# First block's second product on float16 halves, three more steps turned by TensorE, three more copies of V on chip, in a chain of linear attention, FFN and expert FFN

## The chip, the cores and the metric

The program runs on one core of one Trainium2 chip. The metric is the device time of one execution in microseconds: 719.73 us, median of three runs (719.59 to 719.96). Five engines matter: TensorE (PE; its weight loads are shown apart as PEld), VectorE (DVE), ScalarE (ACT), GpSimd (POOL) and SyncE (SP, which issues nearly all transfers).

## The reference

```python
for t in range(S):                       # attention, B=4 H=8 S=768 D=48
    cur = einsum('bhd,bhe->bhde', u * k[t], v[t])
    y[t] = einsum('bhd,bhde->bhe', r[t], state + cur)
    state = w * state + einsum('bhd,bhe->bhde', k[t], v[t])
x = y as [3072, 384]
h = x @ w_in                             # 384 -> 2048
g = maximum(h, 0) + log1p(exp(-abs(h)))
x = g @ w_out                            # 2048 -> 384
logits = x @ w_gate                      # 8 experts, 384 places each, greedy by logit
for e: out[mask_e] = maximum(x[mask_e] @ w1[e], 0) @ w2[e]
```

w_in and w_out arrive as float64 and are turned into float32 on chip.

## The kernel before

**Stages.** The 3072 tokens are 24 attention steps of 128 tokens (two batches of 64 positions), and every three steps make a block of 384 tokens for the FFN, so there are 8 blocks. `attention(n)` scales r and k by powers of w, turns them (L588), multiplies (L615), masks, adds the state (L646 to L660) and writes its 128 rows of x to `xf`. For the FFN x has to stand turned, in `XT`. Steps 0 to 2 are turned by TensorE into float32. The other steps write float16 halves of x to `xhl`, which a DMA with transpose turns (L753). V is needed a second time, in `X`, beside the state: steps 0 to 2 do without it (DIRECT), steps 3 to 5 copy it from the loaded tile on ACT or DVE (`n < COPIED`), from step 6 on a second pair of loads fetches it from HBM (L461).

**Products.** `ffn1(blk, f)` makes g of one of 16 pieces of 128 columns, `ffn2(blk, t, f)` adds one such piece to the output of one step. From block 1 on both work on float16 pairs: a value is hi + lo, and a product is three matmuls (hi·hi, hi·lo, lo·hi; L879 and L1010 to L1012). Block 0 is float32 in both products (L872, L1007): its g is kept whole in `G32`, a view of the memory of the halves, and w_out whole in `WU32`, a view of the memory of the halves one place further on. The 392 columns of L1007 are 384 of w_out and 8 of w_out·w_gate, which `prep_wout` makes (turning w_out by L823, multiplying by L835, turning back by L840).

**Weights.** `from_double` loads float64 pieces (L795, L814; two buffers of 768 KB) and rebuilds float32 by three VectorE operations (L786, L788, L790). `halve_win` (L806) and `halve_wout` (L849) then make the halves, which are needed from block 1 on. Since a half of piece f lies where the float32 of piece f-1 was, halving follows the last use of that.

**Order.** All operations go through a planner, `lay_out`: a list scheduler with a cost for each operation, due times (`due_ffn1`, `due_ffn2` and leads such as HALFL2), and `NUDGE`, a table of numbers that shifts the priority of single operations. Its result is the order of each engine's instructions, which then run in order and wait by semaphores. Where the plan leaves TensorE idle, `keep_warm` puts matmuls of a constant tile (L184, bank 7), which compute nothing that is used; here they are called fillers.

```python
            k = int((it.start - last - 100.0) / step)
            if k > 0 and it.start - last > SWITCH + 60.0:
                        PE.matmul(banks[7][:, :128], still, still, start=True, stop=True)
```

Of the kernel before, what the change touches and what calls it, by code (L numbers as in the profile page):

```python
# [21 lines left out]
def tile_kernel(ctx, tc, r, k, v, w, u, w_in, w_out, w_gate, w1, w2, out):  # L22
# [32 lines left out]
    LAT = 150.0  # L55
    SLACK = 87.403
    SAME = {"dve": 130.0, "act": 150.0}
    NBANK = 7
    BIAS = 1.853
    YIELD0 = 218.503  # L60
    YIELD = {"dve": YIELD0}
# [22 lines left out]
    NUDGE = {  # L84
# [24 lines left out]
    }  # L109
# [219 lines left out]
    TURNED = 3  # L329
    DIRECT = 3  # L330
    SUMMED = 0
    SINGLE = 2
    COPIED = 6
    PARTED = 8
    QUEUES = 1
    UDUE = 2000.0
    ZERODUE = 30000.0
    UTDUE = 6000.0
    HALFL = 12965.117
    HALFL2 = 16904.146  # L340
    NLAT = 6
# [37 lines left out]
    G0 = ffn2p.tile([128, 2, FC, BT], HF, name="g0")  # L379
    G32 = G0.rearrange("p a f t -> p (a f t)").bitcast(FT).rearrange("p (f t) -> p f t", f=FC)  # L380
    G = [[G0[:, 0], G0[:, 1]], several(ffn2p, 2, [128, FC, BT], HF, "g1")]
# [171 lines left out]
    def attention(n):  # L553
# [202 lines left out]
        if blk == 0:  # L756
# [3 lines left out]
            return  # L760
        if n < TURNED:
            op("pe", 1300.0 if summed else 321.0, tx, r=xfs + ["ident"], w=[(a, g, t) for a in ("xh", "xl", "x2")], due=due + 5, bank=b6)
            op(FROM_PSUM, 0.0, lambda eng: scaled(eng, hi, b6.view(KC, 128), 64.0), w=[("xh", g, t)], due=due + 5, bank=b6)
            op("dve", 470.0, lambda: DVE.scalar_tensor_tensor(lo, b6.view(KC, 128), 64.0, hi, op0=OP.mult, op1=OP.subtract),
               r=[("xh", g, t)], w=[("xl", g, t)], due=due + 5, bank=b6)
        else:
            xh, xl = XHL[i][:, :DM], XHL[i][:, DM:]
            op(FROM_SBUF, 0.0, lambda eng: scaled(eng, xh, xf, 64.0), r=[("xf", i)], w=[("xhl", i, 0), "rkT"], due=due + 5)
            op("dve", 470.0, lambda: DVE.scalar_tensor_tensor(xl, xf, 64.0, xh, op0=OP.mult, op1=OP.subtract),
               r=[("xf", i), ("xhl", i, 0)], w=[("xhl", i, 1)], due=due + 5)  # L770
            op("sp", 1340.0, turn, r=[("xhl", i, 0), ("xhl", i, 1)], w=[("xh", g, t), ("xl", g, t), ("x2", g, t)], due=due + 5, size=TURN)
# [72 lines left out]
    def halve_wout(f):  # L844
        due = due_ffn2(1, 0, f) - HALFL2
        hi, lo = WU[:, f, 0], WU[:, f, 1]
        op({"act": 420.0, "dve": 273.0}, 0.0, lambda eng: scaled(eng, hi, WU32[f], 512.0), r=[("wo", f + 1), ("wg", f + 1)],
           w=[("wo", f), ("wg", f)], due=due)
        op("dve", 478.0, lambda: DVE.scalar_tensor_tensor(lo, WU32[f], 512.0, hi, op0=OP.mult, op1=OP.subtract),  # L849
           r=[("wo", f), ("wo", f + 1), ("wg", f + 1)], w=[("wol", f)], due=due)  # L850
# [9 lines left out]
    def ffn1(blk, f):  # L860
# [30 lines left out]
        op("act", 413.0, lambda: ACT.activation(ta, ta, AF.Ln, bias=1.0), w=[("ta", c)], due=due)  # L891
        if blk == 0:
            op("dve", 470.0, lambda: DVE.scalar_tensor_tensor(G32[:, f, :], bank.view(BT), 0.0, ta, op0=OP.max, op1=OP.add),
               r=[("ta", c)], w=[("gh", g, f), ("gl", g, f)], due=due, bank=bank)
            return
        op("dve", 470.0, lambda: DVE.scalar_tensor_tensor(gf, bank.view(BT), 0.0, ta, op0=OP.max, op1=OP.add),  # L896
# [96 lines left out]
    def ffn2(blk, t, late=False):  # L993
# [10 lines left out]
        def mm(f):  # L1004
            p = bank.view(no)
            if blk == 0:
                PE.matmul(p, G32[:, f, ts], WU32[f], start=(f == 0), stop=(f == FC - 1))  # L1007
                return
            gh, gl = G[g]
            PE.matmul(p, gh[:, f, ts], WU[:, f, 0, :no], start=(f == 0), stop=False)  # L1010
            PE.matmul(p, gh[:, f, ts], WU[:, f, 1, :no], start=False, stop=False)  # L1011
            PE.matmul(p, gl[:, f, ts], WU[:, f, 0, :no], start=False, stop=(f == FC - 1))  # L1012

        for f in range(FC):
            it = op("pe", 500.0 if blk else 660.0, lambda f=f: mm(f), r=[(a, g, f) for a in ("gh", "gl")]
               + ([("wo", f), ("wg", f), ("wol", f)] if blk else [("wo", f + 1), ("wg", f + 1)]),
               due=base + 490.0 * (late_n * FC + f) if late else due_ffn2(blk, t, f), bank=bank)
            if blk == 0:
                G0R.append(it)
        scale = 2.0 ** -12 if blk else 4.0  # L1020
        due = base if late else due_ffn2(blk, t, FC - 1)
# [39 lines left out]
    for blk in range(2, NB):  # L1061
        for n in range(blk * SPB, (blk + 1) * SPB):
            load_step(n)
            attention(n)
        for t in range(SPB):
            if (blk - 2, t) not in LATE:
                ffn2(blk - 2, t)
        if blk == 2:
            for f in range(FC):
                halve_wout(f)  # L1070
            gates()
# [559 lines left out]
```

## Time and profile before

| | us |
|---|---|
| median of three runs | 719.73 |
| lowest, highest | 719.59, 719.96 |
| the profiled execution | 720.05 |
| span of its trace | 718.2 |

The profile page gives busy time by engine, then the span in 40 slices of 18 us, then the chain of work that ended last and the costliest groups. A matmul's record is longer than the distance to the next one, since matmuls are pipelined, so a TensorE that is shown busy need not be at its peak. What a matmul costs is read from the starts of consecutive ones. A float32 matmul has two records. The granted clock of TensorE was 0.997 of 2.4 GHz over the span.

### The profile page before, as it was taken

To read this page: it belongs to the slowest core of one execution; us is meant where nothing else is said; L and a number is where in the kernel's file an instruction comes from. 1 tells how busy PE (TensorE), PEld (TensorE's weight loads), DVE (VectorE), ACT (ScalarE), POOL (GpSimd) and SP (SyncE) were. 2 spreads that over 40 slices of the span, in tenths; PEclk is the share of its full clock that TensorE was granted. 3 is DMA by queue.
4 is the path that set the end of the run, shared out by engine and by line. 5 is a ranking of instruction groups with operands and counts; after the bars stand their busy time and mean duration, and the time that the engine had idled before them with its cause. 6 is when DMAs were issued, how large, how long until landed. Compare 5 with 4: busy or idle time off the path is not lost.

```text
span 718.2 us, 18288 instructions
## 1 busy us (share of the span) xinstructions
PE 707.8 (99%) x7173; PEld 458.5 (64%) x7173; DVE 604.0 (84%) x1638; ACT 401.7 (56%) x889; POOL 63.4 (9%) x107
## 2 busy tenths in 40 slices
PE   9999999999899999999999999999999999999996
PEld 8986666657666666666666566666666665566663
DVE  6999999999898968988899868887799898988630
ACT  4588698674398712689999801311345533524530
POOL 3000000000000000000010000001212422313211
PEclk9999999999999999999999999999999999999998
DMA  6985972445741426512010003442358667647900
GB/s 120 267 202 155 237 149 38 90 86 116 124 77 23 74 52 127 75 29 43 15 23 1 1 13 111 122 143 57 102 143 212 192 155 201 195 124 210 265 34 33
DMA packets 165015, 79.65 MB, mean 111 GB/s; under 512 B 132801, under 2 KB 158273, under 8 KB 164929
## 3 DMA queue, kind: packets, MB, share of 16 engines
q1 hardware_dynamic: 159216, 68.56, 42.0%
q0 software_dynamic: 3072, 9.44, 3.7%
q8 instruction: 56, 0.92, 0.5%
q10 hardware_dynamic: 2640, 0.49, 0.4%
q14 instruction: 31, 0.25, 0.1%
HBM read 60.37 MB, written 9.83 MB: 98 GB/s over the span
## 4 chain that ended last, share of the span: by engine, by line
PE 64%; DVE 15%; issue 12%; DMA 3%; POOL 3%; ACT 2%; POOLq 0%; SPq 0%; DVEq 0%
PE bank L879 20%; PE bank L1010 6%; PE bank L1012 6%; PE bank L1011 6%; PE bank L1504 6%; PE bank L1007 3%; DVE ar L625 2%; PE bank L720 2%; PE bank L184 2%; PE bank L1522 2%; PE bank L1524 2%; PE bank L1523 2%; POOL out L1532 2%; PE bank L615 1%; PE bank L588 1%
## 5 line engine op out<-in xcount | busy, mean ns | idle before, releaser
L879 PEld LDWEIGHTS <-wi 128*128 128x128 f16 x1008 | 98.0, 98 | 65.3 <-issue 1.1
L879 PE MATMUL bank<-xt,wi 128*128 128x384 f16 x672 | 127.6, 326 | 0.1
L1010 PE MATMUL bank<-wo,g 128*128 128x384 f16 (+1 forms) x240 | 78.5, 327 | 0.0
L1012 PE MATMUL bank<-wo,g 128*128 128x384 f16 (+1 forms) x240 | 78.5, 327 | 0.0
L1011 PE MATMUL bank<-wo,g 128*128 128x384 f16 (+1 forms) x240 | 78.4, 327 | 0.0
L879 PE MATMUL bank<-xs,wi 128*128 128x384 f16 x336 | 72.9, 326 | 0.0
L1504 PE MATMUL bank<-g,w1h 128*128 128x384 f16 x384 | 72.8, 325 | 0.0
L889 ACT ACTIVATE ta<-bank 128x384 f32<-128x384 f32 x128 | 61.5, 481 | 17.2 <-PE bank L879 12.9
L896 DVE SCALAR_TENSOR_TENSOR gf<-bank,ta 128x384 f32<-128x384 f32 x112 | 61.6, 551 | 11.2 <-ACT ta L891 10.0
L891 ACT ACTIVATE ta<-ta 128x384 f32<-128x384 f32 x128 | 66.6, 522 | 1.7
L890 ACT ACTIVATE ta<-ta 128x384 f32<-128x384 f32 x128 | 66.4, 522 | 1.5
L1524 PE MATMUL bank<-w2h,g 128*128 128x384 f16 x192 | 62.6, 326 | 0.0
L1523 PE MATMUL bank<-w2l,g 128*128 128x384 f16 x192 | 62.5, 326 | 0.0
L1522 PE MATMUL bank<-w2h,g 128*128 128x384 f16 x192 | 62.5, 326 | 0.0
L1508 ACT ACTIVATE g<-bank 128x384 f16<-128x384 f32 x64 | 31.2, 489 | 43.1 <-PE bank L1504 29.2
L421 ACT ACTIVATE x2o<-bank 128x384 f16<-128x384 f32 x23 | 11.3, 493 | 72.8 <-PE bank L1012 65.3
L1504 PEld LDWEIGHTS <-w1h 128*128 128x128 f16 x384 | 35.5, 97 | 22.9 <-issue 1.0
L903 DVE SCALAR_TENSOR_TENSOR g<-gf,g 128x384 f16<-128x384 f32 x80 | 43.2, 549 | 2.9 <-ACT g L421 2.2
L1511 DVE SCALAR_TENSOR_TENSOR g<-bank,g 128x384 f16<-128x384 f32 x64 | 34.4, 547 | 11.0 <-ACT g L1508 11.0
L1504 PE MATMUL bank<-g,w1l 128*128 128x384 f16 x192 | 41.7, 326 | 0.0
L625 DVE TENSOR_TENSOR ar<-bank,mask 64x256 f32<-64x256 f32 x84 | 35.4, 421 | 4.5 <-PE bank L615 2.7
L1429 POOL DMA_INDIRECT third<-x2d,idx x24 | 25.1, 1044 | 150.7 <-PE bank L1317 124.8
(251 smaller groups left out, 1403.9 us busy)
## 6 DMA issues: line engine op xcount, KB each, us to landing
mraw<-moe_w SPq DMA_DIRECT2D x64, 384.0 KB
third<-moe_w_out SPq DMA_DIRECT2D x8, 768.0 KB
third<-moe_w_in SPq DMA_DIRECT2D x6, 768.0 KB
x2d<-x2o SPq DMA_DIRECT2D x48, 96.0 KB
vn<-v SPq DMA_DIRECT2D x47, 96.0 KB
rn<-r SPq DMA_DIRECT2D x46, 96.0 KB
kn<-k SPq DMA_DIRECT2D x46, 96.0 KB
X<-v SPq DMA_DIRECT2D x36, 96.0 KB
```

The lines of the kernel that those rows point to most:

```text
L879: PE.matmul(ph, WF[:, f, a, kk, :], x[:, kk, :], start=(i == 0), stop=(i == 3 * KC - 1))
L889: op("act", 371.0, lambda: ACT.activation(ta, bank.view(BT), AF.Abs), w=[("ta", c)], due=due, bank=bank)
L890: op("act", 413.0, lambda: ACT.activation(ta, ta, AF.Exp, scale=-1.0), w=[("ta", c)], due=due)
L891: op("act", 413.0, lambda: ACT.activation(ta, ta, AF.Ln, bias=1.0), w=[("ta", c)], due=due)
L896: op("dve", 470.0, lambda: DVE.scalar_tensor_tensor(gf, bank.view(BT), 0.0, ta, op0=OP.max, op1=OP.add), r=[("ta", c)], w=[("gf", c)], due ...
L1010: PE.matmul(p, gh[:, f, ts], WU[:, f, 0, :no], start=(f == 0), stop=False)
L1011: PE.matmul(p, gh[:, f, ts], WU[:, f, 1, :no], start=False, stop=False)
L1012: PE.matmul(p, gl[:, f, ts], WU[:, f, 0, :no], start=False, stop=(f == FC - 1))
L1504: PE.matmul(ph, a[:, kk, fs], XH[p][:, x0 + kk, :], start=(i == 0), stop=(i == 3 * KC - 1))
L1522: PE.matmul(po, h1h[:, f, js], w2h[:, fz, :], start=(f == 0), stop=False)
L1523: PE.matmul(po, h1h[:, f, js], w2l[:, fz, :], start=False, stop=False)
L1524: PE.matmul(po, h1l[:, f, js], w2h[:, fz, :], start=False, stop=(f == FB - 1))
```

## The change

Block 0's second product takes the path of the other blocks: `ffn1(0, f)` writes halves of g, `halve_wout` is due before block 0's second product and is laid out ahead of it, and `ffn2(0, t)` is three float16 matmuls a piece. Steps 3 to 5 (block 1) are turned by TensorE and written as halves straight from the bank (the branch that existed for `n < TURNED`). Steps 6 to 8 copy V on chip. Four constants of the planner and the whole table NUDGE are new.

```diff
-    SLACK = 87.403
+    SLACK = 90.403
-    BIAS = 1.853
-    YIELD0 = 218.503
+    BIAS = 1.8750000000000002
+    YIELD0 = 220.503
     NUDGE = {
-        0: -143448, 1: -197030, 4: -22082, 15: -11678, 16: -12043, 17: -29443, 18: -24752, 19: -1000149502, 20: -1000062522, 21: -10145293,
+        1: -10005988, 2: 2036, 4: -24592, 19: -100037979, 20: -999959585, 21: -1000067650, 23: -999932760, 24: -10075748, 43: -10075348, 54:
...
     DIRECT = 3
+    TXPE = 6
-    COPIED = 6
+    COPIED = 9
-    ZERODUE = 30000.0
+    ZERODUE = 120000.0
-    HALFL2 = 16904.146
+    HALFL2 = 5000.0
...
-        if n < TURNED:
+        if n < TXPE:
             op("pe", 1300.0 if summed else 321.0, tx, r=xfs + ["ident"], w=[(a, g, t) for a in ("xh", "xl", "x2")], due=due + 5, bank=b6)
...
     def halve_wout(f):
-        due = due_ffn2(1, 0, f) - HALFL2
+        due = due_ffn2(0, 0, f) - HALFL2
...
-        if blk == 0:
-            op("dve", 470.0, lambda: DVE.scalar_tensor_tensor(G32[:, f, :], bank.view(BT), 0.0, ta, op0=OP.max, op1=OP.add),
-               r=[("ta", c)], w=[("gh", g, f), ("gl", g, f)], due=due, bank=bank)
-            return
...
         def mm(f):
             p = bank.view(no)
-            if blk == 0:
-                PE.matmul(p, G32[:, f, ts], WU32[f], start=(f == 0), stop=(f == FC - 1))
-                return
...
-        scale = 2.0 ** -12 if blk else 4.0
+        scale = 2.0 ** -12
...
+        if blk == 2:
+            for f in range(FC):
+                halve_wout(f)
         for t in range(SPB):
             if (blk - 2, t) not in LATE:
                 ffn2(blk - 2, t)
         if blk == 2:
-            for f in range(FC):
-                halve_wout(f)
             gates()
```

The table sets the order, and its rows tell a reader nothing; three places show what moved. In the changed kernel line numbers differ by three or four: fillers are L187, turning w_out is L826, the three matmuls are L1006 to L1008.

TensorE before, inside block 0's second product (`wo` is w_out, `g` the g of block 0, `identf` the identity matrix): whole products stand between the turning of w_out.

```order
L1007 MATMUL bank_80<-wo,g_127 128x392
L823 MATMUL bank_81<-identf,wo 128x128 x3
L823 MATMUL bank_84<-identf,wo 128x128 x3
L1007 MATMUL bank_86<-wo,g_127 128x392
L835 MATMUL bank_81<-third,gate 32x128 x12
```

TensorE now, where the same product begins: the last of the fillers, then three matmuls for a piece.

```order
L187 LDWEIGHTS still
L187 MATMUL bank_87<-still 128x128
L1006 LDWEIGHTS g_127
L1006 MATMUL bank_81<-wo,g_127 128x392
L1007 LDWEIGHTS g_127
L1007 MATMUL bank_81<-wo,g_127 128x392
L1008 LDWEIGHTS g_127
L1008 MATMUL bank_81<-wo,g_127 128x392
```

Each product of one piece and one step has become three. Between the last matmul of block 0's first product and the first of its second there were 33 fillers, and now there are 117, in ten runs of 5 to 21; in the whole program 204 have become 311.

VectorE before, at the first halving of w_out (`xs`, `wi`: halves and pieces of w_in; `gf`, `ta`: g before it is halved): it stands among the halving of w_in, behind the rebuilding of most of w_out.

```order
L416 TENSOR_TENSOR rs_100<-rn_91,pwn_146 128x8x48
L806 SCALAR_TENSOR_TENSOR third<-wi 128x384
L849 SCALAR_TENSOR_TENSOR wo<-wo 128x392
L423 TENSOR_SCALAR wi<-third 128x384
L423 TENSOR_SCALAR wi<-wi 128x384
L423 TENSOR_SCALAR wo<-wo 128x392
```

VectorE now, at the same halving: it stands among the rebuilding of w_out (L789 to L793) and block 0's g.

```order
L789 TENSOR_SCALAR wo<-third 128x2x384
L426 TENSOR_SCALAR wo<-wo 128x392
L791 SCALAR_TENSOR_TENSOR wo<-third,wo 128x2x384
L809 SCALAR_TENSOR_TENSOR third<-wi 128x384
L793 SCALAR_TENSOR_TENSOR wo<-third,wo 128x2x384
L426 TENSOR_SCALAR wi<-third 128x384
L895 SCALAR_TENSOR_TENSOR gf_126<-bank_83,ta_123 128x384
L852 SCALAR_TENSOR_TENSOR wo<-wo 128x392
```

The halving stood at row 182 of VectorE's list and stands at row 155. In all VectorE has 23 instructions more and ScalarE 21 more.

SyncE before, at the first loads of w_out (`third` holds the float64 pieces, `X` the second copy of V, `vn` the V of a later step): loads of X and of V stand between them.

```order
L795 DMA third<-moe_w_in 128x3x256 x2
L461 DMA X_98<-v 64x8x48 x2
L814 DMA third<-moe_w_out 128x2x768 x2
L461 DMA X_99<-v 64x8x48 x2
L814 DMA third<-moe_w_out 128x2x768
L444 DMA vn_95<-v 64x8x48 x2
```

SyncE now: all eight loads of w_out in a row, and the loads of step 6 behind them.

```order
L798 DMA third<-moe_w_in 128x3x512
L798 DMA third<-moe_w_in 128x3x256 x2
L817 DMA third<-moe_w_out 128x2x768 x8
L447 DMA vn_95<-v 64x8x48 x2
L447 DMA rn_92<-r 64x8x48 x2
L447 DMA kn_94<-k 64x8x48 x2
```

Six loads of X and three transposes by DMA are gone from SyncE's list.

## Rows read from the trace of the kernel before

**Rows 1.** The page: span, busy time by engine, busy tenths in 40 slices.
```profile
span 718.2 us, 18288 instructions
...
PE 707.8 (99%) x7173; PEld 458.5 (64%) x7173; DVE 604.0 (84%) x1638; ACT 401.7 (56%) x889; POOL 63.4 (9%) x107
...
DVE  6999999999898968988899868887799898988630
...
PEclk9999999999999999999999999999999999999998
```

**Rows 2.** Windows: stretch, length, busy us of PE, PEld, DVE, ACT, POOL, then clock, DMA.
```profile
100.00:110.00 10.00, 9.85 (x72) 5.62 (x70) 10.00 (x21) 9.84 (x26) 0.00 (x0) 1.00 0.25 97
...
150.00:160.00 10.00, 10.00 (x99) 6.00 (x98) 9.80 (x27) 6.83 (x17) 0.00 (x0) 1.00 0.35 66
...
180.00:190.00 10.00, 8.31 (x135) 5.10 (x133) 7.54 (x20) 2.43 (x5) 0.00 (x0) 1.00 0.72 115
...
380.00:400.00 20.00, 20.00 (x125) 12.05 (x124) 18.52 (x65) 19.73 (x48) 0.00 (x0) 1.00 0.00 1
```

**Rows 3.** The chain that ended last, by time: start us, us, what.
```profile
69.88 6.14 DMA third<-moe_w_out
...
172.53 2.49 DMA rn<-r
...
181.09 3.09 DMA kn<-k
```

**Rows 4.** Timeline of PE around block 0's second product: start us, us, line, operands, xcount.
```profile
78.00 3.09 PE L1007 MATMUL bank<-wo,g 128*128 128x392 f32 x8
80.92 0.82 PE L823 MATMUL bank<-identf,wo 128*128 128x128 f32 x6
...
123.02 4.77 PE L1007 MATMUL bank<-wo,g 128*128 128x392 f32 x14
127.63 0.33 PE L1010 MATMUL bank<-wo,g 128*128 128x392 f16 x1
...
129.95 0.33 PE L1012 MATMUL bank<-wo,g 128*128 128x392 f16 x1
130.21 0.68 PE L646 MATMUL bank<-vn,ks 64*64 64x48 f32 x32
```

**Rows 5.** Timeline of PE, fillers (L184) and the turning of a step (L750).
```profile
30.75 0.50 PE L750 MATMUL bank<-identf,xf 128*128 128x128 f32 x3
31.08 0.72 PE L184 MATMUL bank<-still 128*128 128x128 bf16 x10
...
72.86 0.90 PE L184 MATMUL bank<-still 128*128 128x128 bf16 x13
73.62 0.85 PE L823 MATMUL bank<-identf,wo 128*128 128x128 f32 x6
```

**Rows 6.** Groups by form: line, engine, operation, xcount, busy us, mean ns of one, idle before.
```profile
L1007 PE MATMUL bank<-wo,g 128*128 128x392 f32 x96 | 35.4, 501 | 0.0
...
L184 PE MATMUL bank<-still 128*128 128x128 bf16 x204 | 16.1, 235 | 1.0 <-DVE wt L479 1.0
...
L903 DVE SCALAR_TENSOR_TENSOR g<-gf,g 128x384 f16<-128x384 f32 x80 | 43.2, 549 | 2.9 <-ACT g L421 2.2
...
L421 ACT ACTIVATE g<-gf 128x384 f16<-128x384 f32 x40 | 20.7, 519 | 2.9 <-DVE gf L896 2.8
...
L427 ACT COPY X<-vn 64x192 f32<-64x192 f32 x12 | 4.2, 349 | 0.2
```

**Rows 7.** Lines L753 and L461 on SP's queue: ns of one, least, median, most.
```profile
L753 SPq DMA_TRANSPOSE xt<-xhl x21: 1211/1279/2962, 49.5 to 370.1; - x21
...
L461 SPq DMA_DIRECT2D X<-v x36: 595/596/2077, 37.7 to 336.6; - x36
```

More of the change, by code (lines that the diff above doesn't have):

```diff
@@ L379, in tile_kernel @@
     G0 = ffn2p.tile([128, 2, FC, BT], HF, name="g0")
-    G32 = G0.rearrange("p a f t -> p (a f t)").bitcast(FT).rearrange("p (f t) -> p f t", f=FC)
     G = [[G0[:, 0], G0[:, 1]], several(ffn2p, 2, [128, FC, BT], HF, "g1")]
@@ L1014, in ffn2 @@
         for f in range(FC):
-            it = op("pe", 500.0 if blk else 660.0, lambda f=f: mm(f), r=[(a, g, f) for a in ("gh", "gl")]
-               + ([("wo", f), ("wg", f), ("wol", f)] if blk else [("wo", f + 1), ("wg", f + 1)]),
+            it = op("pe", 500.0, lambda f=f: mm(f), r=[(a, g, f) for a in ("gh", "gl")]
+               + [("wo", f), ("wg", f), ("wol", f)],
                due=base + 490.0 * (late_n * FC + f) if late else due_ffn2(blk, t, f), bank=bank)
```

49 rows, old and new, of the table NUDGE are left out of this document.

## Prediction

> **What bounds the kernel now.** Read the page first [rows 1]: TensorE is shown busy for 99% of 718.2 us and its clock at full speed in nearly every slice; VectorE is at 84%, but at nine tenths or more in nearly all of slices 2 to 10, that is up to about 180 us. Two engines are full there, so the page cannot say which one waits for the other. The windows tell more [rows 2]: from 100 to 110 us VectorE is busy for 10.00 of 10 us and TensorE for 9.85, from 150 to 160 us 9.80 and 10.00. Only from 180 to 190 us does TensorE show a real hole, 8.31 of 10 us, and VectorE has it too (7.54). From 380 to 400 us TensorE is full beside a VectorE at 18.52 of 20. The chain by time says what the hole is [rows 3]: it runs through a landing of r (2.49 us at 172.53) and one of k (3.09 us at 181.09), loads of an attention step that came late from SyncE's queue; earlier it also runs through a landing of w_out (6.14 us at 69.88). So the time is TensorE's instruction stream, its fillers included, plus a hole of about 1.7 us; and up to 180 us that stream has been laid out against a VectorE without reserve. The change works in just that stretch.
>
> The starts on TensorE give the prices [rows 4, 5]. Fillers are no wait in the records, they are matmuls and count as work. An added filler is therefore to be read as a wait that the new order foresees.
>
> **The change, part by part.** The sum is made against the profiled execution, 720.05 us, which lies 0.32 us above the median of 719.73.
>
> (a) 48 float32 products (16 pieces, 3 steps) go, 144 float16 matmuls come. Seven float32 products in a row take from 123.02 to 127.63 us, 0.66 us each; four take from 78.00 to 80.92, 0.73 us each, with the re-entries from other shapes [rows 4]. The group's 35.4 us of busy time, 0.74 each [rows 6], includes tails that the next work covers. I take 0.69, the middle of the two runs. Three float16 matmuls of 392 columns take 0.50 us (fifteen of them start from 127.63 to 129.95, 0.166 apart). 48 x (0.69 - 0.50) = -9.1 us; bounds -7.7 (0.66) and -11.0 (0.73).
>
> Here a rule of the Trainium skill speaks against the change. The rows show two records for each float32 product and 0.66 us from one product's start to the next. The page Perfetto Trace Analysis, section Engine Utilization, puts TensorE's output rate in float32 at half of the normal one; by that a product would cost two thirds of three float16 matmuls, an estimate of 0.33 us, and (a) would be a loss of 48 x (0.50 - 0.33) = 8.2 us. The rows show about a quarter of the rate of float16 (0.66 beside 0.166 us for 392 columns), so the sum goes by them.
>
> (b) Nine transposes come (three steps of three). Three take from 30.75 to 31.08 us [rows 5], 0.33 us: 3 x 0.33 = +1.0 us. The two operations that write the halves change their source, from `xf` to the bank, and not their number. Three DMA transposes of 1.28 us and six loads of 0.60 us leave SyncE's queue [rows 7], 7.4 us of queue time; nothing else waits on them, and TensorE doesn't gain by that alone.
>
> (c) The order has 107 fillers more, 311 in place of 204 [rows 6]. Thirteen take from 72.86 to 73.62 us, 0.058 each; ten take 31.08 to 31.81, 0.073 each with a gap behind them [rows 5]. I take the tight run: 107 x 0.058 = +6.2 us. 84 of them stand between block 0's first and second product: the second product now has to wait for halves of w_out and of g, which VectorE makes in between, where before it took both whole.
>
> (d) TensorE changes between plain matmuls and those that use slices of the array 137 times, before 125 times (counted in the order). Where L646 follows L1012 the distance is 0.26 us in place of 0.17 [rows 4], 0.09 us lost: 12 x 0.09 = +1.1 us; bounds 0 and +2.5, if the way back costs as much again.
>
> (e) VectorE gets 23 instructions more: 16 third operations of block 0's halves at 0.549 us [rows 6], 8.8 us, and seven others near 0.5 us, together about 12 us by their mean durations. ScalarE gets 15 halvings of g at 0.519 and nine copies of V at 0.349 [rows 6], 10.9 us, and hands others to VectorE. I cost these at nothing beyond (c): what hides them is that the fillers of (c) are placed for these very waits, and that from 200 us on VectorE has reserve to catch up (18.52 of 20 even in a dense window, rows 2). If that cover is too small, it is the third rival.
>
> (f) The hole at 180 to 190 us: the loads that it waits for come off a queue that is 7.4 us emptier by then. Nothing shows how much of the lead reaches them, because a load also waits for its buffer; between 0 and the whole 1.7 us I take half, -0.8 us.
>
> Sum: -9.1 + 1.0 + 6.2 + 1.1 - 0.8 = -1.6 us, 718.45 against the profiled execution, **718.1** against the median: faster by 0.22%, hardly more than the 0.2% (1.44 us) that a measurement of this kernel can tell from no change. Bounds taken together: -11.0 + 1.0 + 6.2 + 0 - 1.7 = -5.5 and -7.7 + 1.0 + 6.2 + 2.5 = +2.0, which is 714.2 and 721.7.
>
> **The rivals.**
>
> 1. *No change.* The hole of (f) stays, because the loads wait for VectorE to free their buffers, and VectorE is later than before. The sum is then -0.8 us: 718.9. For it: VectorE has more to do before 180 us. Against it: the shorter queue. 0.28.
>
> 2. *Clearly faster.* Float32 costs more than I took, since its runs are broken up by transposes (0.73, so -11.0), and the hole closes: -11.0 + 1.0 + 6.2 + 1.1 - 1.7 = -4.4, 715.3. For it: the short runs in [rows 4] are the usual case before 100 us. 0.12.
>
> 3. *Slower: VectorE becomes the bound up to 180 us.* Its 12 us fall into a stretch where it is busy 9.8 to 10.0 of 10 us [rows 2]; only 6.2 us of waits are laid out for it. If TensorE runs out of laid-out work before the halves come, it waits for the other 5.8 us: -0.8 + 5.8 = +5.0, 724.7; with half of the 5.8, 721.8. It decides at the first matmul of block 0's second product, and again where block 1's first product asks for halves of w_in that stand behind those of w_out on VectorE. The Trainium skill's page Perfetto Trace Analysis, section Identifying the Most-Contended Engine, would expect this: TensorE's busy share is not to be trusted, its weight-load share is the better measure, and the engine with the highest occupancy is to be relieved first. The windows agree as far as they go (PEld 5.62 of 10 beside VectorE's 10.00 at 100 us), yet the starts of matmuls 0.166 us apart say that TensorE is full as well. A form of the same: all eight loads of w_out stand in a row, the later ones wait for buffers that VectorE frees, and the loads of step 6 wait behind them. One load of w_out took 6.14 us [rows 3]; if two come late by half of that, the price is about the same 6 us. 0.18 for both.
>
> 4. *The float32 price is half of what I read.* Then 719.73 + 8.2 + 1.0 + 6.2 + 1.1 is 736.2. The rows exclude it nearly: 0.02.
>
> **How the numbers follow.** My forecast has 0.40. Faster by over 0.2%: rival 2 and the forecast less 0.04, as the forecast lies at the edge, 0.12 + 0.36 = 0.48. Within 0.2%: 0.28 + 0.04 = 0.32. Slower: rivals 3 and 4, 0.20. The range goes down to 714.5, near the low sum, and up to 722.4, past the high sum and rival 3 with half of its price; its full price and rival 4 are left out.
>
> **What would show it.** L1006 to L1008 with 392 columns count 144 each, and no float32 product of 392 columns is left. Block 0's second product begins some 3 to 5 us later than at 78.00 us, behind fillers, and its products are 0.50 us apart. VectorE stays at 9.7 or more of 10 us up to about 180 us. Right: from there to the end TensorE has no holes over 1 us, and the last matmul comes 1 to 3 us earlier. Wrong: a real hole of TensorE between 80 and 150 us with VectorE as what ends it (rival 3), a hole at 180 to 190 us with a landing behind it (rival 1), or fillers that are followed at once by work that was long ready, so that they cost more than the wait they stand for.

## The result, and the profile after

The changed kernel takes 723.9 us (median of three, 723.3 to 724.97) where the kernel before took 719.73: ratio 1.0061, 95% interval 1.0045 to 1.0078. The forecast was 718.1 us; the time lies above its range (722.4 at most) and the sign is the other one. The profiled execution of the changed kernel took 724.97 us, the longest of the three, with a span of 723.2; before it was 720.05 and 718.2.

The page of the changed kernel, the lines that answer to [rows 1]:

```profile
span 723.2 us, 18606 instructions
...
PE 710.9 (98%) x7337; PEld 463.5 (64%) x7337; DVE 615.8 (85%) x1660; ACT 406.0 (56%) x884; POOL 63.4 (9%) x107
...
DVE  6899999999999988998799868886889899987630
```

VectorE has 11.8 us more to do, as foreseen, and stays at nine tenths up to about 250 us, not 180. ScalarE, for which the change was said to bring 21 instructions more and term (e) 10.9 us, has 884 in place of 889 on the page and 4.3 us more. Where the 5.0 us of span come from is told by three stretches of TensorE.

**The opening.** Windows of the changed kernel (stretch, length, busy us of PE, PEld, DVE, ACT, POOL, granted clock, DMA):

```profile
22.00:23.00 1.00, 0.00 (x0) 0.00 (x0) 0.59 (x2) 0.00 (x0) 0.00 (x0) 1.00 0.89 180
...
25.00:28.00 3.00, 3.00 (x38) 2.78 (x38) 2.91 (x8) 1.49 (x3) 0.00 (x0) 0.50 1.12 245
```

and its timeline of TensorE at the same place (start, us, line, operands, count, idle before and what ended it):

```profile
20.98 1.00 PE L695 MATMUL bank<-uw,xhl 128*128 128x2 f32 x8
23.18 0.68 PE L649 MATMUL bank<-vn,ks 64*64 64x48 f32 x32 [1.20 <-DMA vn<-v]
...
24.73 2.17 PE L716 MATMUL bank<-X,ar 128*64 128x96 f32 x16
```

TensorE's new order has L649 of step 2 ahead of the outputs of steps 1 and 2. V of step 2 lands only at 23.14 us, TensorE stands for 1.20 us, and then its granted clock is 0.50 for three microseconds (1.2 of 2.4 GHz): sixteen matmuls of L716 take 2.17 us. The kernel before has neither: its outputs of step 1 stand ahead of step 2's V, and its window of 20 to 30 us is full at a clock of 1.00. The prediction had no term for this stretch.

```profile
20.00:30.00 10.00, 10.00 (x229) 9.13 (x230) 9.78 (x22) 4.67 (x11) 0.00 (x0) 1.00 0.95 266
```

**Ahead of block 0's second product.** TensorE's timeline in the changed kernel:

```profile
72.42 0.49 PE L826 MATMUL bank<-identf,wo 128*128 128x128 f32 x3
72.75 0.72 PE L187 MATMUL bank<-still 128*128 128x128 bf16 x10
...
78.02 1.29 PE L187 MATMUL bank<-still 128*128 128x128 bf16 x20
...
80.71 1.34 PE L187 MATMUL bank<-still 128*128 128x128 bf16 x21
...
85.10 0.33 PE L1006 MATMUL bank<-wo,g 128*128 128x392 f16 x1
...
85.64 0.33 PE L1006 MATMUL bank<-wo,g 128*128 128x392 f16 x1
...
86.13 0.33 PE L1006 MATMUL bank<-wo,g 128*128 128x392 f16 x1
```

The second product begins at 85.10 us, 7.1 us later than before [rows 4] and not the 3 to 5 foreseen. Its products are 0.5 us apart, as foreseen. Ahead of it VectorE has no gap: from 69.84 to 84.95 us the chain by time (start, us, what) runs through VectorE alone, which rebuilds and halves w_out and makes g. Its last part:

```profile
81.06 0.87 DVE wo L791
81.93 0.47 DVE third L809
82.40 0.87 DVE wo L793
83.27 0.27 DVE wi L426
83.54 0.47 DVE gf L895
84.01 0.47 DVE wo L852
84.48 0.47 DVE gf L895
```

**The rest.** Windows of the changed kernel, in the columns above:

```profile
180.00:190.00 10.00, 10.00 (x116) 6.26 (x114) 9.81 (x24) 6.93 (x15) 0.00 (x0) 1.00 0.77 147
...
70.00:200.00 130.00, 129.35 (x1555) 85.78 (x1552) 125.89 (x280) 91.31 (x216) 0.82 (x2) 1.00 0.45 99
200.00:420.00 220.00, 219.08 (x2532) 139.27 (x2530) 199.52 (x491) 167.68 (x382) 2.03 (x9) 1.00 0.29 52
```

and the kernel before in two of these windows:

```profile
70.00:200.00 130.00, 128.02 (x1546) 83.27 (x1546) 125.81 (x283) 87.56 (x216) 0.82 (x2) 1.00 0.60 119
200.00:420.00 220.00, 219.91 (x2317) 138.48 (x2316) 188.47 (x471) 165.25 (x392) 2.03 (x9) 1.00 0.24 43
```

The hole at 180 to 190 us [rows 2] is gone. But from 70 to 200 us VectorE was full before and is full now (125.81 and 125.89 us); what it was given there comes out between 200 and 420 us, 199.52 in place of 188.47, and TensorE, which was busy for all but 0.09 us of that stretch, now misses 0.92.

One line marks how far the stream has come: the first and last start of the selection's matmuls (L1265 before, L1262 after) on TensorE. Before:

```profile
L1265 PE MATMUL bank<-oh,cmp x336: 169/176/189, 419.3 to 637.5; 128*128 128x16 bf16 x84, 128*128 128x32 bf16 x84
```

After:

```profile
L1262 PE MATMUL bank<-oh,cmp x336: 168/176/190, 423.5 to 643.2; 128*128 128x16 bf16 x84, 128*128 128x32 bf16 x84
```

4.2 us late at 420, 5.7 at 640.

### The profile page after: what moved, and what is told of

Read it like the earlier page. It is cut to its first block, busy times and chain, and to the rows that moved or that the text cites. A ratio compares the mean times of both kernels' runs of the same rounds, so it can differ in the third digit from the quotient of the medians.

```text
span 723.2 us, 18606 instructions
## 1 busy us (share of the span) xinstructions
PE 710.9 (98%) x7337; PEld 463.5 (64%) x7337; DVE 615.8 (85%) x1660; ACT 406.0 (56%) x884; POOL 63.4 (9%) x107
## 4 chain that ended last, share of the span: by engine, by line
PE 60%; issue 14%; DVE 13%; ACT 5%; POOL 3%; DMA 3%; SPq 1%; POOLq 0%; DVEq 0%; ACTq 0%
PE bank L882 20%; PE bank L1006 7%; PE bank L1008 7%; PE bank L1007 7%; PE bank L1501 4%; PE bank L723 2%; POOL out L1529 2%; PE bank L1519 2%; PE bank L1521 2%; PE bank L1520 2%; PE bank L618 1%; POOL third L1426 1%; PE bank L591 1%; DVE ar L628 1%; PE bank L1262 1%
## 5 line engine op out<-in xcount | busy, mean ns | idle before, releaser
L1006 PE MATMUL bank<-wo,g 128*128 128x392 f16 (+1 forms) x288 | 94.5, 328 | 0.0
L1008 PE MATMUL bank<-wo,g 128*128 128x392 f16 (+1 forms) x288 | 94.3, 327 | 0.0
L1007 PE MATMUL bank<-wo,g 128*128 128x392 f16 (+1 forms) x288 | 94.2, 327 | 0.0
L895 DVE SCALAR_TENSOR_TENSOR gf<-bank,ta 128x384 f32<-128x384 f32 x128 | 69.7, 552 | 8.1 <-ACT ta L894 7.0
L892 ACT ACTIVATE ta<-bank 128x384 f32<-128x384 f32 x128 | 60.9, 479 | 16.1 <-PE bank L882 13.2
L893 ACT ACTIVATE ta<-ta 128x384 f32<-128x384 f32 x128 | 65.8, 520 | 1.8
L894 ACT ACTIVATE ta<-ta 128x384 f32<-128x384 f32 x128 | 65.5, 519 | 1.6
L902 DVE SCALAR_TENSOR_TENSOR g<-gf,g 128x384 f16<-128x384 f32 x96 | 52.2, 550 | 2.9 <-ACT g L424 2.4
L1460 DVE SCALAR_TENSOR_TENSOR w2l<-mraw,w2h 128x768 f16<-128x768 f32 x32 | 30.2, 952 | 13.1 <-ACT w2h L1456 9.8
L1008 PEld LDWEIGHTS <-g 128*128 128x128 f16 x288 | 28.1, 98 | 19.4 <-issue 0.2
```

The source lines that it names most:

```text
L892: op("act", 371.0, lambda: ACT.activation(ta, bank.view(BT), AF.Abs), w=[("ta", c)], due=due, bank=bank)
L893: op("act", 413.0, lambda: ACT.activation(ta, ta, AF.Exp, scale=-1.0), w=[("ta", c)], due=due)
```

## The experiments

Each run is compared with the kernel before on the same chip, whose medians there were 718.73 to 719.85 us; so the ratio counts. 0.0014 of it is 1 us. Theory A: the opening makes the loss. Theory B: VectorE (with ScalarE) paces TensorE, and its extra work costs time. Theory C: the fillers themselves are the loss. Theory D: the parts are good, their new order is bad. Theory E: VectorE's work is put off, and TensorE pays after 200 us.

**1. The opening put right.** A table gives the instructions of the first 24.5 us the engine and place that they had before; all else stays.

```diff
-        assert len(order) == len(todo)
+        assert len(order) == len(todo); opening(order, every)
```

> The changed kernel, with the instructions that the kernel before runs in its first 24.5 us put back into the order of the kernel before on every engine; all that follows keeps the changed order. Theory A (the opening makes the loss): TensorE's wait for step 2's V at 22 to 23 us and the low granted clock behind it (0.92, 0.50 and 0.87 from 24 to 29 us) go, and with them about 3.3 us: 720 to 721 us. Theory B (VectorE paces TensorE up to about 105 us, so that what is won earlier is only waited for later): the granted clock stays at 1.00 from 20 to 29 us as well, but the time falls by 1 us or less: 723 to 724 us.

Measured: 721.88 us, ratio 1.0044 (1.0030 to 1.0058); by the profiled spans 2.2 us less than the changed kernel (721.0), by the ratios 1.2, with intervals that overlap. The window and the start of the second product in this run:

```profile
25.00:28.00 3.00, 3.00 (x56) 2.71 (x53) 2.90 (x8) 2.00 (x4) 0.00 (x0) 1.00 0.98 242
```

```profile
82.51 0.33 PE L1006 MATMUL bank<-wo,g 128*128 128x392 f16 x1
```

The clock stays at 1.00 and the second product begins 2.6 us sooner. By the traces the selection begins 1.2 us sooner than in the changed kernel (422.3 against 423.5) and ends 2.2 sooner (641.0 against 643.2). Theory A holds for one to two of the 4.2 us. That nothing of it arrives, as B has it, is against the traces, though the ratios alone would allow it. The rest is not the opening.

**2. Without fillers, and without VectorE's work too.** The 117 fillers ahead of the second product are left out; in the second run also the second of the three operations that rebuild w_out, in the third run the same on the kernel before.

```diff
-            if k > 0 and it.start - last > SWITCH + 60.0:
+            if k > 0 and it.start - last > SWITCH + 60.0 and not 66000.0 < last < 81000.0:
```

> The changed kernel without the 117 fillers that stand in TensorE's order between the end of block 0's first product (72 us) and the start of its second product (85 us); they take about 6.5 us there. If they only fill real waits for VectorE (theory B), the first matmul of the second product starts at 84.5 to 85.2 us as before, VectorE is named as what ends the waits, and the time is 723 to 725 us. If the fillers themselves are the loss (theory C: more of them than there is to wait), the second product starts 2 to 6 us sooner and the time falls to 718 to 722 us. A fall of the granted clock in the new holes would make it slower than 725 us.

> As the run without the 117 fillers, and the second of the three operations that rebuild w_out on VectorE is left out (8 of 0.95 us, 0.87 us apart, so 7.0 us of VectorE's time between 66 and 105 us; w_out loses its signs). Theory B (VectorE paces that stage): 3 to 7 us less than the run without fillers, 717 to 721 us. Theory C or a bound by the loads: within 1 us of the run without fillers.

> The control: the kernel before without its 33 fillers between 71.8 and 77.4 us, and without the same 8 operations on VectorE (w_out loses its signs there too). If VectorE paces both kernels alike up to 105 us, this falls by 3 to 7 us as well, to 713 to 717 us. If it is the change that made VectorE the bound, the kernel before gains 2 us at most: 717.5 to 720 us.

Measured: 725.9 us (1.0090, 1.0062 to 1.0118), 725.3 us (1.0098, 1.0064 to 1.0131) and 718.11 us (0.9986, 0.9977 to 0.9995). In the first of them TensorE waits where the fillers were, and the clock falls. Timeline and windows of that run:

```profile
75.78 0.55 PE L826 MATMUL bank<-identf,wo 128*128 128x128 f32 x3 [0.57 <-DVE g L902]
76.89 0.68 PE L826 MATMUL bank<-identf,wo 128*128 128x128 f32 x3 [0.57 <-ACT third L430]
```

```profile
75.00:80.00 5.00, 3.86 (x48) 2.54 (x46) 5.00 (x11) 3.60 (x9) 0.00 (x0) 0.72 0.65 208
80.00:85.00 5.00, 3.76 (x29) 2.78 (x26) 5.00 (x10) 4.19 (x11) 0.00 (x0) 0.50 0.50 157
```

With the clock at half, these two cannot tell B from C; that needed the runs of part 5. The control gains 1.0 us for 7.0 us of VectorE's time, within its bound of 2. Even without fillers TensorE is busy there for 10.00 of 10 us from 60 to 70 us and 8.68 from 70 to 80, the likely reason why taking work off VectorE alone brings little.

**3. The parts alone, in the order of the kernel before.** The planner sees the items of the kernel before, so that every engine keeps its order; new instructions are put in behind the one that they depend on, ahead of their first user. The product's part, for instance:

```diff
+        behind.append(Behind("act", 413.0, lambda: it.done + 150.0, lambda: scaled("act", gh, gf, 32.0), users))
+        behind.append(Behind("dve", 470.0, lambda: hi.done + 150.0, lambda: DVE.scalar_tensor_tensor(gl, gf, 32.0, gh, op0=OP.mult, op1=OP.subtract), users))
```

> The kernel before in its own order on every engine, with the first of the three parts alone: block 0's second product from fp16 halves (144 matmuls where 48 float32 products were), the halves of g written on ScalarE and VectorE right behind the instruction that wrote g in float32, those of w_out right behind the copy of the gate's columns, 16 ScalarE and 32 VectorE instructions earlier than before or new. Theory D (the part is good, the change's new order loses it): 48 x 0.166 us = 8.0 us less on TensorE, of which at least 5 arrive: 711 to 714 us. Theory B (block 0's product now waits for VectorE's halves, in whatever order): 718 to 723 us, with TensorE's waits between 77 and 115 us ended by VectorE's or ScalarE's halves of w_out or g.

> The kernel before in its own order, with the second part alone: steps 3 to 5 are turned by nine TensorE transposes from fp32 into a PSUM bank, and three DMA transposes are gone. 1.0 us more on TensorE (the price in the prediction), as many VectorE and ScalarE instructions as before: 719 to 721 us by every theory; under 718.5 us the DMA transposes themselves had held something up.

> The kernel before in its own order, with the third part alone: V of steps 6 to 8 is copied on ScalarE (12 copies), and six loads leave SyncE's queue. If the hole at 180 to 190 us comes from loads that land late behind these, it shrinks and the time falls by up to 1.7 us: 717.5 to 719 us. If the hole has another cause, the time stays within 0.7 us of the kernel before.

> The copies of V for steps 6 to 8 in the kernel before's order again, but each placed in ScalarE's queue directly ahead of its user instead of where the load stood: in the first such run ScalarE waited 4.2 us at 93 us for V that had not landed, and TensorE with it. If the six loads' leaving SyncE's queue is worth something, as the prediction's term of -0.8 us for the hole at 180 to 190 us says: 717.5 to 719.5 us. If not: 719.5 to 722 us.

> The kernel before in its own order, with all three parts: what the change computes and issues, without its new order. Theory D (the new order is what made it slower): the sum of the three parts, 711 to 716 us. Theory B (the halves of block 0 are what made it slower): 719 to 724 us, near the changed kernel's time.

Measured: product 735.14 us (1.0231, 1.0218 to 1.0244); turns 720.95 (1.0032, 1.0022 to 1.0041); copies 723.77 (1.0067, 1.0054 to 1.0081), better placed 721.7 (1.0035, 1.0022 to 1.0047); all 736.24 (1.0263, 1.0242 to 1.0283). Each part is a loss in the old order, and the product's is 16 us. From 70 to 200 us its waits on TensorE (what waited, what ended it, us, times, longest) and the window of 60 to 70 us:

```profile
PE bank L1033 <- DVE wo L853: 5.7, 12, 1.2
PE bank L1032 <- ACT wo L422: 1.9, 2, 1.3
```

```profile
60.00:70.00 10.00, 7.54 (x66) 4.34 (x65) 10.00 (x23) 7.95 (x18) 0.00 (x0) 1.00 0.60 173
```

TensorE stands for the halves (in this kernel's numbering L1032 to L1034 are the product's matmuls, L422 and L853 the upper and lower half of w_out), and already at 60 to 70 us, before any second product, since VectorE is late with block 0's first one. Theory D falls for these places, the nearest to hand; other places were not tried. Against them the change's own order is worth 14.5 us to the parts (1.0263 against 1.0061). The first copies run measured something else than it was meant to: ScalarE's queue stood for V, and TensorE behind it (ScalarE's and TensorE's timelines):

```profile
91.25 0.71 ACT L428 COPY X<-vn 64x192 f32<-64x192 f32 x2 [4.06 <-DMA vn<-v]
```

```profile
93.10 0.48 PE L850 MATMUL bank<-identf,third 128*128 128x128 f32 x1 [4.16 <-ACT third L428]
```

The second one, without that wait, shows the hole a window further on:

```profile
180.00:190.00 10.00, 10.00 (x162) 6.37 (x154) 7.12 (x19) 1.02 (x2) 0.00 (x0) 1.00 1.00 104
190.00:200.00 10.00, 7.92 (x152) 5.86 (x151) 9.80 (x24) 4.71 (x12) 0.00 (x0) 1.00 0.66 131
```

So the six loads that leave the queue do not close it by themselves. That in the changed kernel it is the order that does is argued and not shown: in the product's run, in the old order, TensorE has 9.69 and 10.00 of 10 us in these two windows, so a stream that comes later is a rival.

**4. The price of VectorE's time.** One more VectorE operation, read by nobody, behind each of the 16 that write block 0's g in the kernel before; then the product's part again with its 32 lower halves on GpSimd.

```diff
+ DVE.scalar_tensor_tensor(gf, ta, 32.0, ta, op0=OP.mult, op1=OP.subtract)
```

> The price of VectorE's time in the kernel before, measured alone: behind each of the 16 instructions that write g of block 0, one more VectorE operation of the same size (what a half of g costs: 16 x 0.47 us = 7.5 us between 43 and 78 us), whose output nobody reads; nothing else is changed. Theory B (VectorE paces this stage): 5 to 8 us more, 724 to 728 us, with TensorE's new holes between 45 and 80 us ended by VectorE. If VectorE has slack there, as the prediction took it when it costed the new instructions at nothing beyond the fillers: within 1.5 us of the kernel before.

> As the run of the fp16 product alone in the kernel before's order (735.1 us), but the lower halves of g and of w_out are made on GpSimd, idle at this time, with two operations each (64 in all). Theory B (VectorE's 32 halves are what cost 16 us there): at least 8 us come back, 719 to 727 us; if GpSimd takes under 1 us for a half, even less than the kernel before: 712 to 719 us. If the wait is for the chain gate, ScalarE's half, lower half, whoever makes it: 732 us or more. GpSimd's time for an operation of this size is not in any trace so far.

Measured: 725.2 us (1.0085, 1.0071 to 1.0099): 7.5 us on VectorE cost 6.1 us of time. The window of 60 to 70 us and the longest wait (L872 is block 0's first product, L790 the last of the operations that rebuild a piece of w_in):

```profile
60.00:70.00 10.00, 7.92 (x64) 4.43 (x63) 10.00 (x23) 6.06 (x14) 0.00 (x0) 0.83 0.50 144
```

```profile
PE bank L872 <- DVE wi L790: 2.1, 1, 2.1
```

Theory B is right about the kernel before: VectorE has no slack here. Part of the 6.1 us is the clock, which was 0.83 in this window, that is 1.2 GHz for about 3.4 of its 10 us; as an estimate from this, at most 1.7 us. On GpSimd the halves were no help: 760.81 us (1.0578). Its groups:

```profile
L879 POOL TENSOR_SCALAR gf<-gf 128x384 f32<-128x384 f32 x16 | 21.6, 1351 | 44.1 <-ACT g L422 44.1
L879 POOL TENSOR_TENSOR g<-gf,g 128x384 f16<-128x384 f32 x16 | 17.0, 1062 | 1.3
```

A lower half of g takes 2.4 us there, and TensorE waited 24.2 us for those of w_out; its granted clock was 0.968 over the span (0.997 before), so that part of the time is the clock's. The Trainium skill's page GPSIMD Engine Reference, section Engine selection, advises against it for operations with two inputs, about twice VectorE's time; the trace agrees (1.06 beside 0.55 us).

**5. Are the fillers real waits, and is it VectorE in the new order?** On the changed kernel: block 0's lower halves of g left out (the third matmul reads the upper half). On the changed kernel with the opening put right: half of the 117 fillers, a quarter of them, and half of them without those lower halves.

```diff
-            k = int((it.start - last - 100.0) / step)
+            k = int((it.start - last - 100.0) / step) // (2 if 66000.0 < last < 81000.0 else 1)
```

> The changed kernel in its own order without the 16 VectorE operations that make the lower halves of block 0's g (the third matmul of block 0's second product reads the upper half instead): 7.5 us less for VectorE between 45 and 85 us, all fillers kept. Theory B (VectorE paces the changed kernel there): the first product's end comes forward from 72 us and the time falls by 2 to 6 us: 717 to 721 us (what the fillers hold cannot come forward). If VectorE's extra work is hidden: within 1 us of the changed kernel, 722.5 to 725 us.

> The changed kernel with the opening of the kernel before (721.9 us), and 61 of the 117 fillers ahead of block 0's second product taken out (every row of them cut by half); the rest should keep TensorE's clock at 1.00. Theory B (the 117 stand for real waits for VectorE and ScalarE): the second product still starts 12.5 to 12.7 us after the first transpose of w_out, and the time stays within 1 us, 721 to 723 us. Theory C (the order holds more fillers than there is to wait; without any of them TensorE's waits up to the half clock came to 3 us): the second product starts 2.5 to 3.4 us sooner, 718.5 to 719.5 us, level with the kernel before.

> The same with 92 of the 117 fillers taken out. Theory B: as the run with half of them, waits in their place. Theory C: 3 to 5 us less than with all (717 to 719 us) if the clock holds at 1.00; if it falls to 0.50 in the holes, as it did with none, 720 to 724 us.

> As the run with half of the fillers, and without the 16 VectorE operations for the lower halves of block 0's g (the third matmul reads the upper half instead): 7.5 us less for VectorE. If what is left of the wait ahead of the second product is VectorE's (theory B), 1.5 to 4 us less than the run with half of the fillers; if it is the way from the transposes over ScalarE's copies and the gate to the halves of w_out, within 1 us of it.

Measured: 723.36 us (1.0058, 1.0039 to 1.0077); 722.93 (1.0043, 1.0027 to 1.0058); 723.46 (1.0050, 1.0037 to 1.0064); 722.55 (1.0038, 1.0025 to 1.0050). The last three cannot be told from the run with all fillers (1.0044). With a quarter of the fillers, from the first turning of w_out to the second product:

```profile
69.93 0.49 PE L826 MATMUL bank<-identf,wo 128*128 128x128 f32 x3
...
70.99 0.55 PE L826 MATMUL bank<-identf,wo 128*128 128x128 f32 x3 [0.46 <-ACT third L430]
...
82.52 0.33 PE L1006 MATMUL bank<-wo,g 128*128 128x392 f16 x1
```

That is 12.59 us, and 12.68 with all of them (72.42 to 85.10): the fillers stand for real waits. Theory C falls. With half of them and 7.5 us less for VectorE:

```profile
69.42 0.49 PE L826 MATMUL bank<-identf,wo 128*128 128x128 f32 x3
...
81.56 0.33 PE L1006 MATMUL bank<-wo,g 128*128 128x392 f16 x1
```

12.14 us, 0.45 less. So g's lower halves hold the start up by no more than that. It would be wrong to read from this that VectorE does not pace the new order. Followed back from the product's first matmul in the run with a quarter of the fillers, TensorE (at L618) waits until 81.54 us for VectorE's L895, and VectorE has no gap from there back to before the turning. In the run without the lower halves the same way back goes to ScalarE's copies (L430) and from there between them and the turning of w_out, and VectorE, busy for 10.00 of 10 us from 70 to 80 us in the other run, is busy for 8.68. Two ways are nearly of one length, and taking work off VectorE alone gains the 0.45 us by which its own is longer. Nor does this reach the later stretch: from 200 to 420 us VectorE is busy for 199.23 us in the first of these four runs and for 199.52 in the changed kernel, so its added work there is what the order puts there, not a queue that has run over.

**6. After 200 us.** Without the lower halves of g of blocks 3 and 4, 15 us of VectorE's time, on the changed kernel with the opening put right and on the kernel before (the third matmul reads the upper half).

```diff
-        op("dve", 470.0, rest, r=[("gh", g, f)]
+        op("dve", 470.0, rest if blk not in (3, 4) else lambda: None, r=[("gh", g, f)]
```

> The changed kernel with the opening of the kernel before (721.9 us), without the 32 VectorE operations that make the lower halves of g of blocks 3 and 4 (the third matmul of their second product reads the upper half instead): 15.0 us less for VectorE between 200 and 335 us, where VectorE is busy for 11 us more than in the kernel before. Theory E (VectorE's added work is only put off, and TensorE pays for it between 200 and 420 us): TensorE's waits there go, 718.5 to 720.5 us. If that work lies beside TensorE's there: within 0.7 us, 721 to 722.7 us.

> The control: the kernel before without the same 32 operations. By theory E TensorE has next to no waits there (219.91 of 220 us busy), so it gains nothing: within 0.7 us of the kernel before. If it gains as much as the changed kernel, theory E is not supported.

Measured: 722.39 us (1.0039, 1.0025 to 1.0052) and 719.59 us (0.9994, 0.9984 to 1.0005). By the total, theory E fails: nothing gained over 1.0044 that can be told. The windows say more. The run with the opening put right, then this one:

```profile
200.00:420.00 220.00, 218.41 (x2525) 138.83 (x2524) 199.14 (x492) 166.52 (x380) 2.03 (x9) 1.00 0.29 51
420.00:640.00 220.00, 219.62 (x1752) 135.71 (x1750) 188.42 (x655) 71.11 (x118) 35.79 (x46) 1.00 0.51 139
```

```profile
200.00:420.00 220.00, 219.82 (x2550) 140.03 (x2549) 185.93 (x464) 165.33 (x377) 2.03 (x9) 1.00 0.28 51
420.00:640.00 220.00, 218.27 (x1738) 134.50 (x1735) 186.46 (x648) 71.68 (x119) 36.51 (x46) 1.00 0.51 139
```

TensorE wins 1.41 us before 420 and loses 1.35 after it. The first is clear of chance: the changed kernel and the seven other runs in its order that leave blocks 3 and 4 alone show 218.41 to 219.20 us in this stretch. The selection begins at 419.7 us in place of 422.3 and ends its last round at 640.1 in place of 641.0; there TensorE waits for VectorE's compares:

```profile
PE bank L1262 <- DVE cmp L1247: 1.4, 3, 0.7
```

So VectorE's put-off work does make TensorE wait between 200 and 420 us, and what is saved there is mostly given back in the selection; what holds the selection is not shown. The run with half of the fillers did the same: the selection began 2.0 us sooner than with all (420.3) and ended no sooner (641.2).

## Why the prediction was wrong

**Failed: the second half of (e).** It put VectorE's 12 us "at nothing beyond (c): what hides them is that the fillers of (c) are placed for these very waits, and that from 200 us on VectorE has reserve to catch up". The first cover held: the stretch is 12.6 us with the fillers or with waits in their place. The second did not: VectorE took the 11 us into 200 to 420 us, where its mean over the stretch had room (188.47 of 220) but single waits did not, and TensorE lost 0.8 us more there than before, 1.5 in the run with the opening put right. Its price was there to be had: 7.5 us more on VectorE cost the kernel before 6.1 us, the clock's part included.

**Failed: no term for the opening.** The prediction read the new order around block 0's second product only. The moved L649, the landing of V behind it and the clock cost 2.2 us by the profiled spans, 1.2 by the ratios.

**(a)** The size is right. Counted on TensorE from each matmul's start to the next one's (to its own end where a wait follows), the 48 float32 products took 33.1 us, 0.69 each, and the 144 matmuls in their place 25.1, 0.52 for three with the re-entries among them: 8.0 us less, what (a) and (d) make together (-9.1 + 1.1). The rule of the Trainium skill (Perfetto Trace Analysis, Engine Utilization) by which float32 would run at half the rate would have made a product dearer after than before; the starts exclude it, as [rows 4] did.

**(b)** was +1.0; alone in the old order it measured +2.3 (0.0032 of 718.73), though the profiled run of it has the span of the kernel before (718.1 us). Counted in the same way the transposes take 0.9 us more in the changed kernel; where the rest of the 2.3 goes is open.

**(c)** was +6.2; the group's busy time grew by 7.1 us (16.1 in [rows 6], 23.2 after), from start to start by 6.4. Right in what it meant: not idle turning, but waits.

**(d)** was not tried by itself; see (a).

**(f)** The hole closed wholly, -1.7 and not -0.8, but not for the reason given: with the six loads gone in the old order it only moved on. Nor is its size fixed: in the last control, whose order up to there is that of the kernel before, TensorE is busy for 9.20 of these 10 us and not 8.31, so about half of the 1.7 us belongs to the one trace.

**Rival 3** had the sign and nearly the size (724.7), by half of its mechanism: VectorE has no slack, but at 85 us this shows as the fillers that (c) had counted and as a later start, and as a wait only after 200 us. The Trainium skill's page Perfetto Trace Analysis, section Identifying the Most-Contended Engine, judges TensorE by its weight loads and not by its busy share, and relieves the engine with the highest occupancy first; by [rows 1] that is VectorE. The runs agree: the change relieves TensorE by some 8 us and loads VectorE, and the run that loads VectorE alone costs 6.1 us.

In the sum: -2.5 us was due with the hole closed (-9.1 + 1.0 + 6.2 + 1.1 - 1.7), +5.0 came by the spans, 7.5 apart. Counted from start to start as in (a), the terms themselves came as forecast: products -8.0, transposes +0.9, fillers +6.4. Beside them stand 1.5 us for the half clock at the opening (L713 and L716), and waits of TensorE that are 1.8 us longer in all though the hole of 1.7 is gone, so 3.5 us of new ones: 1.2 at the opening, 0.6 in the first 10 us, 0.8 between 200 and 420 us, 0.9 elsewhere. The last 2.3 us are spread over the other matmuls, no group by more than 0.7; why they stand further apart is open. So of the miss 2.7 us are the opening's, about 1 is VectorE's put-off work, and half stays without a cause that a run has shown.

## What to carry to other kernels

When two engines are both full, a price on one of them has to be set for the other too: load it with a dummy operation and measure, before work is traded from the one to the other. To take work off it and gain nothing does not show that it had slack; a second way may be as long. Read a new order from its first instruction, not only where the arithmetic changed; and where instructions fill time on purpose, take them out by half to see whether a wait stands beneath. A gain inside a stage counts only if the next stage can start from it.

## What was not expected of the hardware

One wait of 1.20 us on TensorE at 22 us, after and before small matmuls, was followed by three microseconds at a granted clock of 0.50. With a quarter of the fillers kept, TensorE was idle for about a third of 70 to 80 us (busy 6.73 of 10), in pieces of up to 0.8 us, and the clock stayed at 1.00; with none it fell to 0.72 and 0.50. How deep it fell at the opening was not the same in all runs: 0.83 over 20 to 30 us in the changed kernel, 0.66 in the run without fillers, with the same order up to there.
